# Packing four attention heads into TensorE, wider exponentials and hand-sliced background work in a two-layer attention and FFN kernel

## The chip, the cores and the metric

One core of one Trainium2 chip. The metric is the device time of one execution, in microseconds (us). Most executions of one kernel agree within 0.3%, those of the changed kernel within 0.5%; exceptions are named. Engines: PE is TensorE (PEld its weight loads), ACT is ScalarE, DVE is VectorE, POOL is GpSimd. PSUM is the memory that matmuls write to; a bank of it holds 512 columns here. The granted clock is the share of TensorE's full clock that the profile records; in all traces of this case the record is either 1 or 0.5. "Start to start" below is the distance between the starts of two neighbouring instructions of one engine; it is the cost of one of them in a full stream.

## The reference

```python
def _A_ref(x, wqkv, wo):            # S = 2048, D = 512, H = 32 heads of Dh = 16
    qkv = ...                       # x @ wqkv, split into q, k, v per head
    scores = jnp.einsum("bhqd,bhkd->bhqk", q, k) * Dh ** -0.5
    o = jnp.einsum("bhqk,bhkd->bhqd", _softmax(scores), v)
    return ... @ wo
def _B_ref(x, w1, w2):              # F = 1792
    return _silu(x @ w1) @ w2       # written as einsums
x = A_x
x = x + _A_ref(_layernorm(x), A_wqkv, A_wo)
x = x + _B_ref(_layernorm(x), B_w1, B_w2)
x = x + _A_ref(_layernorm(x), A_wqkv, A_wo)
x = x + _B_ref(_layernorm(x), B_w1, B_w2)
```

The heads have only 16 dimensions, so the scores and the weighted values of 32 heads fill little of a 128x128 array, while every score needs an exponential: 2 x 32 x 2048 x 2048 of them, 128 at a time.

## The kernel before

A query chunk is 512 tokens. For each pair of heads and each of 16 key tiles: two score matmuls (all 128 rows of the array; the query copy QJ has zeros in the rows of the other heads), one exponential of 1024 columns, two value matmuls whose weights are 128 columns wide, of which 17 are used (the 17th is a column of ones: the softmax sum).

```python
def emit_s(kt, ...):
    s_ps = psr.s_tile(kt % 2).rearrange("p (a b) -> p a b", a=2)
    for jj in range(2):
        nc.tensor.matmul(s_ps[:, jj, :], lhsT=KT[:, _hb, kt * P : (kt + 1) * P],
                         rhs=_qtj[:, jj, :], start=True, stop=True)
# [cut]
for kt in range(NKT):
    s_ps = s_tiles.pop(kt)
    p_sb = ppool.tile([P, 2, 512], BF16, name="p_sb", tag="p")
    nc.scalar.activation(p_sb[:]..., s_ps[:]..., ACT.Exp, scale=float(SCALE))
    if kt + 2 < NKT:
        emit_s(kt + 2)
    for jj in range(2):
        h = 4 * hb + 2 * pr + jj
        nc.tensor.matmul(o_ps[:, jj, :], lhsT=vaug[:, kt, 17 * h : 17 * h + P],
                         rhs=p_sb[:, jj, :], start=(kt == 0), stop=(kt == NKT - 1))
```

Projections, norms and the FFN of the chunk before are ordinary code; a scheduler interleaves them. The norms' square root runs on ACT in some places. A bound on each row's score is subtracted through an extra row (Bm, amax).

Of the kernel before, what the change touches and what calls it, by code (L numbers as in the profile page):

```python
# [8 lines left out]
ACT = mybir.ActivationFunctionType  # L9
ALU = mybir.AluOpType  # L10
AX = mybir.AxisListType
FP32 = mybir.dt.float32
BF16 = mybir.dt.bfloat16


@with_exitstack
def kernel(
# [11 lines left out]

# [4 lines left out]
    P = 128  # L34
    H = 32
    DH = D // H
    assert D == 512 and DH == 16, (D, DH)
    assert S % 512 == 0 and F % P == 0
    CT = D // P
    TT = S // P  # L40
    NQC = S // 512
    FT = F // P
    HB = H // 4
    NKT = TT
    SCALE = DH ** -0.5
    EPS = 1e-5

    cpool = ctx.enter_context(tc.tile_pool(name="cpool", bufs=1))
    wpool = ctx.enter_context(tc.tile_pool(name="wpool", bufs=1))
    xpool = ctx.enter_context(tc.tile_pool(name="xpool", bufs=1))  # L50
    xnpool = ctx.enter_context(tc.tile_pool(name="xnpool", bufs=4))
    xtpool = ctx.enter_context(tc.tile_pool(name="xtpool", bufs=4))
    qtpool = ctx.enter_context(tc.tile_pool(name="qtpool", bufs=2))
    qwork = ctx.enter_context(tc.tile_pool(name="qwork", bufs=1))
    ppool = ctx.enter_context(tc.tile_pool(name="ppool", bufs=3))
    otpool = ctx.enter_context(tc.tile_pool(name="otpool", bufs=1))
    achunk_pool = ctx.enter_context(tc.tile_pool(name="achunk", bufs=2))
    atpool = ctx.enter_context(tc.tile_pool(name="atpool", bufs=2))
    htpool = ctx.enter_context(tc.tile_pool(name="htpool", bufs=1))
    tpool = ctx.enter_context(tc.tile_pool(name="tpool", bufs=1))  # L60
    lnpool = ctx.enter_context(tc.tile_pool(name="lnpool", bufs=2))
    small = ctx.enter_context(tc.tile_pool(name="small", bufs=4))
    pspool = ctx.enter_context(tc.tile_pool(name="pspool", bufs=1, space=bass.MemoryType.PSUM))
    PSF = pspool.tile([P, 4096], FP32, name="PSF")
    PSBF = PSF[:].bitcast(BF16)

    class _PSRegions:
        def __init__(self):
            self.g_ctr = 0

        def s_tile(self, idx):
            return PSF[:, idx * 1024 : (idx + 1) * 1024]

        def o_tile(self):
            return PSF[:, 2048:3072].rearrange("p (a b) -> p a b", a=2)

        def att_tile(self):
            return PSBF[:, 4096:5120].rearrange("p (a b c) -> p a b c", a=4, b=2)

        def g_f32(self):  # L80
            i = self.g_ctr % 2
            self.g_ctr += 1
            return PSF[:, 3072 + 512 * i : 3072 + 512 * (i + 1)]

        def g_bf16_ct(self):
            i = self.g_ctr % 2
            self.g_ctr += 1
            base = 6144 + 1024 * i
            return PSBF[:, base : base + CT * P].rearrange("p (a b) -> p a b", a=CT)

    psr = _PSRegions()


    ident = cpool.tile([P, P], BF16, name="ident")
    make_identity(nc, ident[:])
    cw = cpool.tile([P, 768], BF16, name="cw")
    nc.vector.memset(cw[:], 0.0)
    nc.vector.memset(cw[0:1, 128:640], 1.0)
    for j in range(4):
        nc.vector.memset(cw[0:1, 32 * j + 16 : 32 * j + 17], 1.0)  # L100
        nc.vector.memset(cw[0:1, 640 + 32 * j : 640 + 32 * j + 16], 1.0)
    E = cpool.tile([P, P], BF16, name="E")
    nc.gpsimd.memset(E[:], 0.0)
    for j in range(4):
        nc.gpsimd.memset(E[32 * j : 32 * j + 16, 32 * j + 16 : 32 * j + 17], -1.0)
    eps_t = cpool.tile([P, 1], FP32, name="eps_t")
    nc.vector.memset(eps_t[:], EPS)

    onescol = cpool.tile([P, 1], FP32, name="onescol")
    maskcol = cpool.tile([P, 1], FP32, name="maskcol")  # L110
    mc_ps = psr.g_f32()
    nc.tensor.matmul(mc_ps[:, 0:1], lhsT=cw[0:1, 0:128], rhs=cw[0:1, 128:129], start=True, stop=True)
    nc.tensor.matmul(mc_ps[:, 2:3], lhsT=cw[0:1, 640:768], rhs=cw[0:1, 128:129], start=True, stop=True)
    nc.vector.tensor_copy(out=onescol[:], in_=mc_ps[:, 0:1])
    nc.vector.tensor_copy(out=maskcol[:], in_=mc_ps[:, 2:3])

    x_sb = xpool.tile([P, TT, D], BF16, name="x_sb")
    for c in range(NQC):
        nc.sync.dma_start(
            x_sb[:, 4 * c : 4 * c + 4, :],  # L120
            xf[512 * c : 512 * (c + 1), :].rearrange("(tt p) d -> p tt d", p=P),
        )

    wq_pad = wpool.tile([P, CT, HB, P], BF16, name="wq_pad")
    wk_pad = wpool.tile([P, CT, HB, P], BF16, name="wk_pad")
    wv_sb = wpool.tile([P, CT, D], BF16, name="wv_sb")
    wo_sb = wpool.tile([P, CT, D], BF16, name="wo_sb")
    w1_sb = wpool.tile([P, CT, F], BF16, name="w1_sb")
    w2_sb = wpool.tile([P, FT, D], BF16, name="w2_sb")

    def _qk_src(ct, col0):
        return bass.AP(
            tensor=A_wqkv.tensor,
            offset=A_wqkv.offset + (ct * P) * 3 * D + col0,
            ap=[[3 * D, P], [16, 32], [1, 32]],
        )

    for ct in range(CT):
        nc.sync.dma_start(
            out=wk_pad[:, ct, :, :].rearrange("p hb (j s) -> p (hb j) s", s=32),  # L140
            in_=_qk_src(ct, D),
        )
    for ct in range(CT):
        nc.sync.dma_start(
            out=wq_pad[:, ct, :, :].rearrange("p hb (j s) -> p (hb j) s", s=32),
            in_=_qk_src(ct, 0),
        )
    nc.sync.dma_start(
        wv_sb[:], A_wqkv[:, 2 * D : 3 * D].rearrange("(ct p) f -> p ct f", p=P)
    )  # L150
# [4 lines left out]
    KT = xpool.tile([P, HB, S], BF16, name="KT")  # L155
    VW = 17 * (H - 1) + P + 17
    VW = (VW + 31) // 32 * 32
    vaug = xpool.tile([P, TT, VW], BF16, name="vaug")
    nc.vector.memset(vaug[:, :, 16 * H : VW], 1.0)
    nc.vector.memset(  # L160
        vaug[:, :, 0 : 17 * H].rearrange("p t (h e) -> p t h e", e=17)[:, :, :, 16:17],
        1.0,
    )
    QJs = [
        [xpool.tile([P, 2, 512], BF16, name=f"QJ{pr}{b}") for b in range(2)]
        for pr in range(2)
    ]
    for pr in range(2):
        for b in range(2):
            nc.vector.memset(QJs[pr][b][:], 0.0)  # L170
    qj_ctr = [0, 0]
    Bm = xpool.tile([P, HB, P], BF16, name="Bm")
    amax = xpool.tile([P, HB], FP32, name="amax")
    amaxp = xpool.tile([P, HB, NQC], FP32, name="amaxp")
    hT = htpool.tile([P, FT, 512], BF16, name="hT")

    def ln_tiles(tts, act_sqrt=True):
        n = len(tts)
        mvb = lnpool.tile([P, n, 2], FP32, name="mvb", tag=f"mvb{n}")
        for i, tt in enumerate(tts):  # L180
            st = lnpool.tile([P, 6], FP32, name="st", tag="st", bufs=4)
            nc.vector.bn_stats(st[:], x_sb[:, tt, :])  # L182
            nc.vector.bn_aggr(mvb[:, i, :], st[:])  # L183
        rstd = lnpool.tile([P, n, 1], FP32, name="rstd", tag=f"rstd{n}")
        if act_sqrt:
            std = lnpool.tile([P, n, 1], FP32, name="std", tag=f"std{n}")
            nc.scalar.activation(  # L187
                std[:], mvb[:, :, 1:2], ACT.Sqrt, bias=eps_t[:], scale=1.0
            )
            nc.vector.reciprocal(rstd[:], std[:])  # L190
        else:
            a = lnpool.tile([P, n, 1], FP32, name="lna", tag=f"lna{n}")
            nc.vector.tensor_scalar_add(out=a[:], in0=mvb[:, :, 1:2], scalar1=float(EPS))
            r = lnpool.tile([P, n, 1], FP32, name="lnr", tag=f"lnr{n}")
            nc.vector.reciprocal(out=r[:], in_=a[:])
            rh = lnpool.tile([P, n, 1], FP32, name="lnrh", tag=f"lnrh{n}")
            nc.vector.tensor_scalar_mul(out=rh[:], in0=r[:], scalar1=0.5)
            nc.vector.tensor_scalar(
                out=rstd[:], in0=r[:], scalar1=1.0, scalar2=0.5, op0=ALU.add, op1=ALU.mult
            )  # L200
            rec = lnpool.tile([P, n, 1], FP32, name="lnrec", tag=f"lnrec{n}")
            t = lnpool.tile([P, n, 1], FP32, name="lnt", tag=f"lnt{n}")
            for _ in range(11):
                nc.vector.reciprocal(out=rec[:], in_=rstd[:])
                nc.vector.tensor_tensor(out=t[:], in0=rec[:], in1=rh[:], op=ALU.mult)
# [17 lines left out]
    def ln_chunk(qc, act_sqrt=True):  # L223
        return ln_tiles([4 * qc + i for i in range(4)], act_sqrt=act_sqrt)
# [371 lines left out]
```

## Time and profile before

| what | value |
|---|---|
| time, median of 12 runs | 2551.56 us (2549.15 to 2554.52) |
| PE busy, share of the span | 93% |
| ACT busy | 79% |
| exponentials | 2048 of 1024 columns, 1918 us, idle 362 us before them |
| granted clock | 0.991 |

How to read it: PE and ACT are idle little, and nearly tie. The question for the change is which of the two a removed piece of work belongs to, and what the other then does. The lines are in the prediction.

### The profile page before, as it was taken

How to read it: one execution, taken by the hardware profiler on the slowest of the kernel's cores; microseconds unless marked ns; L12 is line 12 of the kernel's file. 1: busy time of each engine (PE TensorE's matmuls, PEld its weight loads, DVE VectorE, ACT ScalarE, POOL GpSimd, SP SyncE). 2: the span in 40 equal slices, each digit the busy share in tenths (PEclk: the TensorE clock that was granted, in tenths of full speed). 3: DMA queues.
4: the chain of work that ended last, by engine and by line, in shares of the span. 5: the costliest groups of instructions: out<-in, count | busy, mean ns of one | idle time of the engine just before them, and what ended most of it. 6: DMA issues, size and time to landing. Idle time of an engine off the chain costs nothing.

```text
span 2551.0 us, 28923 instructions
## 1 busy us (share of the span) xinstructions
PE 2373.3 (93%) x11204; PEld 1054.8 (41%) x11426; DVE 828.3 (32%) x1841; ACT 2010.5 (79%) x2196; POOL 1.2 (0%) x11
## 2 busy tenths in 40 slices
PE   5999999999999989999689999999999999999997
PEld 2444444444444434444234444444444444344443
DVE  8233332312432142311573233423123411413124
ACT  1887789997789959999327877899968999499981
POOL 0000000000000000000000000000000000000000
PEclk9999999999999999999889999999999999999999
DMA  8000000000000000000000000000000000000000
GB/s 140 1 1 1 1 1 1 1 1 1 1 1 1 1 1 1 1 1 1 0 1 1 1 1 1 1 1 1 1 9 1 1 1 1 9 1 1 1 1 17
DMA packets 40650, 12.87 MB, mean 5 GB/s; under 512 B 33088, under 2 KB 40000, under 8 KB 40512
## 3 DMA queue, kind: packets, MB, share of 16 engines
q1 hardware_dynamic: 40512, 11.01, 2.3%
q8 instruction: 89, 1.46, 0.2%
q14 instruction: 49, 0.40, 0.1%
HBM read 8.91 MB, written 2.10 MB: 4 GB/s over the span
## 4 chain that ended last, share of the span: by engine, by line
PE 64%; ACT 21%; DVE 11%; issue 4%; ACTq 0%
PE PSF L354 26%; PE PSF L379 23%; ACT p_sb L369 20%; PE PSF L458 4%; PE PSF L296 2%; PE PSF L391 2%; PE PSF L437 2%; PE PSF L242 2%; DVE hT L446 1%; DVE st L182 1%; ACT t_sb L445 1%; PE PSF L420 1%; DVE oT L387 1%; PE PSF L281 1%; DVE KT L249 1%
## 5 line engine op out<-in xcount | busy, mean ns | idle before, releaser
L369 ACT ACTIVATE p_sb<-PSF 128x1024 bf16<-128x1024 f32 x2048 | 1918.1, 1044 | 362.1 <-PE PSF L354 283.9
L354 PE MATMUL PSF<-QJ,KT 128*128 128x512 bf16 x4034 | 1202.6, 378 | 41.8 <-ACT p_sb L369 22.7
L379 PE MATMUL PSF<-p_sb,vaug 128*128 128x512 bf16 x3970 | 1170.8, 378 | 5.7 <-ACT p_sb L369 0.3
L354 PEld LDWEIGHTS <-KT 128*128 128x128 bf16 x4096 | 396.4, 97 | 584.7 <-issue 272.4
L379 PEld LDWEIGHTS <-vaug 128*128 128x128 bf16 x4096 | 397.1, 97 | 490.8 <-issue 47.0
L387 DVE CAST oT<-PSF 128x1024 bf16<-128x1024 f32 x128 | 156.7, 1224 | 622.4 <-PE PSF L379 622.4
L344 DVE COPY QJ<-QT 17x512 bf16<-17x512 bf16 x256 | 72.7, 284 | 611.3 <-PE PSF L354 606.8
L437 PE MATMUL PSF<-xnT,w_sb 128*128 128x512 bf16 x442 | 135.5, 395 | 23.0 <-DVE hT L446 21.1
L445 ACT ACTIVATE t_sb<-PSF 128x512 f32<-128x512 f32 x112 | 67.2, 600 | 54.0 <-DVE hT L446 37.7
L458 PE MATMUL PSF<-w_sb,hT 128*128 128x512 bf16 x440 | 97.6, 379 | 3.5 <-DVE hT L446 3.1
L446 DVE SCALAR_TENSOR_TENSOR hT<-t_sb,PSF 128x512 bf16<-128x512 f32 x112 | 76.9, 687 | 56.1 <-ACT t_sb L445 55.7
L249 DVE TENSOR_SCALAR KT<-PSF,maskcol,onescol 128x512 bf16<-128x512 f32 x64 | 50.6, 807 | 125.0 <-PE PSF L242 124.5
L296 PE MATMUL PSF<-xnT,wq_pad 128*128 128x512 bf16 x246 | 73.0, 381 | 17.0 <-DVE qtmp L304 10.8
L391 PE MATMUL PSF<-ident,oT 128*128 128x128 bf16 x1024 | 78.4, 219 | 10.5 <-DVE oT L387 9.8
L242 PE MATMUL PSF<-xnT,wk_pad 128*128 128x512 bf16 x250 | 73.6, 397 | 14.3 <-DVE KT L249 6.8
L391 PEld LDWEIGHTS <-oT 128*128 128x128 bf16 x1024 | 65.1, 98 | 48.1 <-DVE oT L387 26.6
L187 ACT ACTIVATE std<-mvb,eps_t 128x4 f32<-128x4 f32 x16 | 4.8, 297 | 96.5 <-DVE mvb L183 96.5
L437 PEld LDWEIGHTS <-w_sb 128*128 128x128 bf16 x448 | 44.8, 100 | 86.3 <-issue 42.7
L231 PE MATMUL PSF<-ident,xn 128*128 128x128 bf16 x352 | 38.0, 252 | 42.1 <-DVE xn L212 33.1
L458 PEld LDWEIGHTS <-hT 128*128 128x128 bf16 x448 | 43.8, 98 | 57.3 <-issue 5.3
L304 DVE CAST qtmp<-PSF 128x512 bf16<-128x512 f32 x64 | 44.2, 690 | 48.8 <-PE PSF L296 45.7
L182 DVE BATCH_NORM_STATS2 st<-x_sb 128x6 f32<-128x512 bf16 x88 | 58.8, 676 | 0.4
(58 smaller groups left out, 660.6 us busy)
## 6 DMA issues: line engine op xcount, KB each, us to landing
w_sb<-in_B_w_dram SPq DMA_DIRECT2D x2, 1792.0 KB, 11.8
x_sb<-in_A_x_dram SPq DMA_DIRECT2D x4, 512.0 KB, 5.7
out_dram<-x_sb SPq DMA_DIRECT2D x4, 512.0 KB, 2.9
wk_pad<-in_A_wqkv_dram SPq DMA_DIRECT2D x4, 256.0 KB, 9.6
wq_pad<-in_A_wqkv_dram SPq DMA_DIRECT2D x4, 256.0 KB, 8.8
wv_sb<-in_A_wqkv_dram SPq DMA_DIRECT2D x1, 512.0 KB, 6.5
wo_sb<-in_A_wo_dram SPq DMA_DIRECT2D x1, 512.0 KB, 4.9
```

The lines of the kernel that those rows point to most:

```text
L182: nc.vector.bn_stats(st[:], x_sb[:, tt, :])
L242: nc.tensor.matmul(k_ps[:, :], lhsT=wk_pad[:, ct, hb, :], rhs=xnT[:, ct, :], start=(ct == 0), stop=(ct == CT - 1),)
L296: nc.tensor.matmul(q_ps[:, :], lhsT=wq_pad[:, ct, hb, :], rhs=xnT[:, ct, :], start=(ct == 0), stop=(ct == CT - 1),)
L354: nc.tensor.matmul(s_ps[:, jj, :], lhsT=KT[:, _hb, kt * P : (kt + 1) * P], rhs=_qtj[:, jj, :], start=True, stop=True,)
L369: nc.scalar.activation(p_sb[:].rearrange("p a b -> p (a b)"), s_ps[:].rearrange("p a b -> p (a b)"), ACT.Exp, scale=float(SCALE),)
L379: nc.tensor.matmul(o_ps[:, jj, :], lhsT=vaug[:, kt, 17 * h : 17 * h + P], rhs=p_sb[:, jj, :], start=(kt == 0), stop=(kt == NKT - 1),)
L387: nc.vector.tensor_copy(out=oT[:, :, :], in_=o_ps[:, :, :])
L391: nc.tensor.transpose(att_ps[:, tq, jj, :], oT[:, jj, tq * P : (tq + 1) * P], ident[:, :],)
L437: nc.tensor.matmul(h_ps[:, :], lhsT=w1_sb[:, ct, ft * P : (ft + 1) * P], rhs=xnT[:, ct, :], start=(ct == 0), stop=(ct == CT - 1),)
L445: nc.scalar.activation(t_sb[:], h_ps[:, :], ACT.Tanh, scale=0.5)
L446: nc.vector.scalar_tensor_tensor(out=hT[:, ft, :], in0=t_sb[:], scalar=1.0, in1=h_ps[:, :], op0=ALU.add, op1=ALU.mult,)
L458: nc.tensor.matmul(y_ps[:, :], lhsT=hT[:, ft, tq * P : (tq + 1) * P], rhs=w2_sb[:, ft, :], start=(ft == 0), stop=(ft == FT - 1),)
```

## The change

Intent: let neighbouring heads use different parts of the array at once, so that PE stops limiting, and let ACT run without a gap on wider instructions. Its core, cut, with remarks added after #:

```diff
+    NB = 3                                  # blocks of 512 columns per exponential
-                            lhsT=KT[:, _hb, kt * P : (kt + 1) * P],
-                            rhs=_qtj[:, jj, :],
+                r = slice(32 * j, 32 * j + 32)          # j: one of four row groups
+                    s_ps[:, i, :],                      # i: one of three banks
+                    lhsT=KT[L, kt // 4][r, g, (kt % 4) * P : (kt % 4 + 1) * P],
+                    rhs=QT[L, qc][r, g, par, :],
-                            o_ps[:, jj, :],
-                            lhsT=vaug[:, kt, 17 * h : 17 * h + P],
+                o_ps[32 * j : 32 * j + 32, :],          # one of four column groups
+                lhsT=VA[L, kt // 4][:, kt % 4, 17 * h : 17 * h + 32],
... [cut: pools; scores of tile t are issued, then values of tile t - 2, then the exponential of t]
+            if not (urgent or late):
+                if bg.queue:
+                    bg.pump()               # one slice of projection, norm or FFN work
+                else:                       # nothing to do: two dummy matmuls
+                    d_ps = ps_m.tile([P, 512], FP32, name="d_ps", tag="m")
+                    for _ in range(2):
+                        nc.tensor.matmul(d_ps[:], lhsT=ident[:], rhs=w1_sb[:, 0, 0:512], ...)
... [cut]
+    def m_tile(shape, dt, name):            # "burst": work that exponentials wait for
+        if burst[0]:                        # may use three rotating PSUM tiles
+            burst[1] += 1
+            if burst[1] % 3:
+                return ps_s.tile(shape, dt, name=name, tag="s")
+        return ps_m.tile(shape, dt, name=name, tag="m")
-            nc.scalar.activation(std[:], mvb[:, :, 1:2], ACT.Sqrt, bias=eps_t[:], scale=1.0)
+        nc.gpsimd.tensor_scalar_add(rstd[:], mv[:, :, 1:2], float(EPS))
+        nc.gpsimd.tensor_tensor(out=rstd[:], in0=rstd[:], in1=half[:], op=ALU.pow)
```

Below, a "tile" is one exponential with its score and value matmuls, and a "slice" is the piece of background work that one tile may carry (two matmuls or four transposes). When a group of four heads ends, the kernel finishes the background accumulation that is under way, because there is only one bank for both.

## The prediction

> **What bounds the kernel now.** I read the busy shares first, then the chain that ended last, then the costliest groups. These are the busy line, the chain's engines and the three large groups:
>
> ```profile
> PE 2373.3 (93%) x11204; PEld 1054.8 (41%) x11426; DVE 828.3 (32%) x1841; ACT 2010.5 (79%) x2196; POOL 1.2 (0%) x11
> ...
> PE 64%; ACT 21%; DVE 11%; issue 4%; ACTq 0%
> ...
> L369 ACT ACTIVATE p_sb<-PSF 128x1024 bf16<-128x1024 f32 x2048 | 1918.1, 1044 | 362.1 <-PE PSF L354 283.9
> L354 PE MATMUL PSF<-QJ,KT 128*128 128x512 bf16 x4034 | 1202.6, 378 | 41.8 <-ACT p_sb L369 22.7
> L379 PE MATMUL PSF<-p_sb,vaug 128*128 128x512 bf16 x3970 | 1170.8, 378 | 5.7 <-ACT p_sb L369 0.3
> ```
>
> Two engines are nearly tied. ScalarE's exponentials need 1918 us and idle 362 us, mostly waiting for the score matmuls; TensorE's busy time is 93% of the span. The timeline separates them. First ScalarE, then TensorE in a stretch of pure attention:
>
> ```profile
> 403.21 2.85 ACT L369 ACTIVATE p_sb<-PSF 128x1024 bf16<-128x1024 f32 x3 [0.26 <-PE PSF L354]
> ...
> 604.57 12.11 ACT L369 ACTIVATE p_sb<-PSF 128x1024 bf16<-128x1024 f32 x13 [0.38 <-PE PSF L379]
> ```
>
> ```profile
> 607.48 0.59 PE L354 MATMUL PSF<-QJ,KT 128*128 128x512 bf16 x2
> ...
> 607.91 0.59 PE L379 MATMUL PSF<-p_sb,vaug 128*128 128x512 bf16 x2
> ...
> 608.40 0.59 PE L354 MATMUL PSF<-QJ,KT 128*128 128x512 bf16 x2
> ```
>
> Three exponentials whose scores are ready take 2.85, so one costs (2.85 - 1.04)/2 = 0.903 us start to start. In the longer run it is (12.11 - 1.04)/12 = 0.922, because one step of TensorE, two score and two value matmuls, repeats every 0.92 us (607.48 to 608.40). A matmul costs (0.59 - 0.378) = about 0.215, so four cost 0.86: the tie. Any projection or FFN matmul put into such a step makes TensorE the bound, and that is where the 362 us of ScalarE idle time come from.
>
> Last, the stretches without attention: start, boundary between the layers, tail.
>
> ```profile
> 0.00:62.00 62.00, 35.34 (x175) 17.87 (x179) 54.97 (x141) 6.00 (x10) 1.17 (x11) 1.00 0.83 144
> ...
> 1205.00:1322.00 117.00, 87.13 (x405) 39.73 (x411) 75.76 (x166) 26.33 (x37) 0.00 (x0) 0.87 0.00 1
> ...
> 2476.00:2551.00 75.00, 54.87 (x249) 23.95 (x252) 31.98 (x57) 15.86 (x25) 0.00 (x0) 0.95 0.04 15
> ```
>
> Columns: stretch, length, busy time of PE, weight loads, DVE, ACT and POOL, granted clock, DMA share, GB/s. Together 254 us in which ScalarE works 48.
>
> **What the Trainium skill says.** (1) "ScalarE: Activation LUTs", What ACT_TABLE_LOAD costs: an ACTIVATE with immediate operands takes 186 ns + 0.833 ns per column, back-to-back ones overlap by 93 ns, and exp and tanh share a table set. The trace agrees on length (186 + 853 = 1039; measured 1044) and on the set (tables are reloaded only around the square root). The overlap is larger here: 1044 - 903 = 141 ns. So a start-to-start cost is about 50 ns + 0.833 per column. (2) "TensorE: Matmul & The Clock Gate", Part 3: a K=32 matmul takes as long as a K=128 one; the gain is concurrency of matmuls at different row groups (four gave 3.07x) or at different column groups (three gave 2.38x). No matmul of the kernel before is packed, so its trace cannot confirm it. (3) "TensorEngine Tiling (Array Packing)", Key Properties: changing the tiling mode drains the engine. Not shown before either. (4) The first of these TensorE pages, Part 1: an idle window of about 3.4 us halves the clock. The boundary's 0.87 agrees.
>
> **The change part by part.** The change rewrites the kernel; the arithmetic of the attention stays 4096 blocks (8 chunks x 32 heads x 16 key tiles) of 128x512 scores.
>
> Exponentials: 2048 instructions of 1024 columns become 1365 of 1536 and one of 512. By (1): 50 + 1280 = 1.33 us each, 1365 x 1.33 + 0.5 = 1816 us, against 2048 x 0.903 = 1849 if before had never waited. So wider instructions give only 33 us; the rest must come from ScalarE no longer waiting.
>
> TensorE: each score matmul now uses 32 rows (keys of one head, zeros masked in the query), three neighbours at three row groups into three banks; each value matmul has 32 columns, three neighbours at different column groups of one bank. Packed by (2), a triple should cost about its full length, 0.38 + 0.01. With a drain after scores, values and background by (3), a tile costs 0.39 + 0.39, plus a background step of two matmuls (0.215 + 0.378 = 0.59): 1.37 us at worst, equal to an exponential; without a background step 0.78. Background matmuls: K and Q now handle eight heads instead of four, so 256 + 256 become 128 + 128, and the 64 of the bound (Bm) vanish; V, output and FFN keep 128 + 128 + 896. That is 1408 instead of 1728. Transposes (eight in a row took 0.61 us, 0.08 each) fall from 1504 to 640. In total per tile (1408 x 0.215 + 640 x 0.08)/1366 = 0.26 us on average, so TensorE has room.
>
> Background work in slices: each tile pumps one slice (two matmuls or eight transposes). I count per chunk about 12 slices for the output projection, 79 for the FFN, 25 for the next layer's LN, K and V, 12 for Q, with their gaps, and some 20 tiles where a group's end takes the place: 148 of the 171 tiles. So it fits, with few idle slots (there the dummy matmuls run). 84 of 112 tanh land between exponentials, 0.05 + 0.427 = 0.48 each: 40 us.
>
> VectorE: the absolute maximum (42 us), the |q| and bound operations (44 + 48) and the QJ copies (73) go; output casts become 64 of 512 columns (0.69 each) for 128 of 1.224. Far from the bound. LN's square root goes to a power on GpSimd: 20 table loads of 1.28 us become one, mostly in the boundary anyway.
>
> Start: before, the first exponential starts at 58.6 us, after K weights arrive in 64-byte pieces and after LN of all chunks. Now one x chunk, then one wide weight transfer (estimate 11 us, from the 11.8 that 1792 KB took), LN of one chunk about 6 us beside it, K, Q, V: first exponential at about 20. Chunks 1 to 3 still need LN, K and V (about 9 us of VectorE: 2.6 statistics, 1.4 normalising, 1.5 copies, 5 x 0.69) before their keys; two tiles of exponentials hide some: 3 x 8 = 24 us lost.
>
> Boundary: layer 2 starts on the three finished chunks, and after 16 tiles needs the fourth's FFN, LN, K and V in one burst. The FFN's first half now costs 1.41 us per group of 128, as in the tail:
>
> ```profile
> 2521.30 1.02 PE L437 MATMUL PSF<-xnT,w_sb 128*128 128x512 bf16 x4 [0.39 <-DVE hT L446]
> ...
> 2521.34 0.60 ACT L445 ACTIVATE t_sb<-PSF 128x512 f32<-128x512 f32 x1 [0.81 <-DVE hT L446]
> ...
> 2521.97 0.69 DVE L446 SCALAR_TENSOR_TENSOR hT<-t_sb,PSF 128x512 bf16<-128x512 f32 x1 [0.72 <-ACT t_sb L445]
> ...
> 2522.71 1.02 PE L437 MATMUL PSF<-xnT,w_sb 128*128 128x512 bf16 x4 [0.39 <-DVE hT L446]
> ```
>
> With three rotating PSUM tiles instead of two, the 0.39 wait should shrink: 14 x 1.0 = 14, second half 56 x 0.215 = 12, two LN of 6 to 7, K and V 8 x 0.87 = 7, less two hidden tiles: about 45 us. Tail: output projection 7, LN 6, 14 + 12, last add and store 4, group end 2: about 45.
>
> Sum: 20 + 1816 + 40 + 24 + 45 + 45 = 1990. Add 64 group ends at about 0.2 (13) and about 700 matmul slices that each overrun ScalarE by 1.37 - 1.33 = 0.04 (28): 2031 us, ratio 0.796.
>
> **The rivals.** Rival A, no concurrency: triples run one after another at 0.215. Then TensorE needs (8192 + 1408) x 0.215 + 51 = 2115, plus dummies in perhaps 160 tiles (70) and 60 to 80 us in which it is idle at the ends: about 2260. For: no trace here shows packing. Against: the skill's measured ratios, and operands that start at partitions 0, 32, 64, 96. Even so faster by 11%.
> Rival B, drains and weight loads cost more than I gave, say 0.25 us more per tile: TensorE becomes the bound in the about 900 tiles with slices and loses 0.25 x 900 = 220 us, about 2220. For: three mode changes per tile. Against: the score tiles are made a whole exponential ahead, so slices with gaps give time back.
> Rival C, the clock halves because of gaps: a tile costs 2.7, span far above 2551 if permanent. Against: TensorE would be idle less than 1 us at a time, and the dummies fill empty slots; only the burst and the tail (LN) are exposed, some 10 us.
> Rival D, everything is absorbed better than I think (no group end cost, no overrun, shorter bursts): 1960.
>
> **Range and chances.** Mine and D hold about 75%, A and B together 20%, C 3%. Predicted 2030, 8 in 10 between 1960 and 2150. A loss of all gain needs C or something unseen: faster 0.95, within 2% 0.02, slower 0.03.
>
> **What would show it.** Right: exponentials of 128x1536 with a mean near 1.46 us, 1.33 apart, their idle time falling from 362 to about 150 us, nearly all in start, boundary and tail; ScalarE above 90% of the span; three score matmuls starting within about 0.1 us of each other; chain led by ACT. Wrong: score starts 0.215 apart (A); gaps before value matmuls and exponentials waiting for scores in ordinary tiles (B); granted clock well under 0.95 outside the ends (C); first exponential long after 20 us or a boundary above 60 us (my sums of the serial parts).

## The result, and the profile after

The changed kernel takes 2085.2 us (median of 8 runs, 2082.64 to 2093.21). The ratio is 0.8174 (95% interval 0.8164 to 0.8184). Ratios here are the mean time of one kernel's fast runs over the mean time of the other's fast runs in the same rounds, so not quite the ratio of the medians.

From the page after, the busy line, the clock row (tenths of full speed, 40 slices of the span), the chain by engine, and the four large groups:

```profile
PE 1739.8 (84%) x11072; PEld 586.2 (28%) x11266; DVE 415.4 (20%) x746; ACT 1904.1 (92%) x1479; POOL 36.4 (2%) x47
...
PEclk8999998889989899999979999999998999989999
...
ACT 56%; issue 23%; PE 16%; DVE 4%; POOL 1%; DMA 0%; ACTq 0%; POOLq 0%
...
L496 ACT ACTIVATE p_sb<-s_ps 128x1536 bf16<-128x1536 f32 x1366 | 1861.7, 1735 | 120.8 <-PE s_ps L479 120.3
L479 PE MATMUL s_ps<-QT,KT 32*128 32x512 bf16 x4096 | 564.1, 400 | 221.3 <-ACT p_sb L496 155.2
L420 PE MATMUL o_ps<-p_sb,VA 128*32 128x512 bf16 x4096 | 587.3, 411 | 1.6 <-DVE oT L429 1.4
L508 PE MATMUL d_ps<-w_sb,ident 128*128 128x512 bf16 x944 | 293.4, 385 | 0.0
```

ACT now leads the chain and is 92% busy; its idle time before exponentials fell from 362 to 121 us. The same 4096 score and 4096 value matmuls keep PE busy for 564 and 587 us in place of 1203 and 1171. The last line is the dummies: 293 us of work that computes nothing. And the clock row is no longer all 9: its mean is 0.934 against 0.991.

An ordinary tile on PE, with dummies, in layer 2:

```profile
1137.81 0.39 PE L479 MATMUL s_ps<-QT,KT 32*128 32x512 bf16 x3
...
1138.13 0.40 PE L420 MATMUL o_ps<-p_sb,VA 128*32 128x512 bf16 x3
...
1138.46 0.61 PE L508 MATMUL d_ps<-w_sb,ident 128*128 128x512 bf16 x2
...
1139.15 0.39 PE L479 MATMUL s_ps<-QT,KT 32*128 32x512 bf16 x3
```

Three packed matmuls together last as long as one (0.39). The three scores of a tile start within 0.01 us of each other, in all tiles of this trace: the packing does run them at once. The next kind starts 0.32 us after them, not 0.215 after as a matmul of the same kind does: about 0.11 us is lost at each change of shape. What in the change costs this, no run separates. Two full-array dummies take 0.54 (the weight loads of the next scores are recorded at 1139.00; the scores themselves then wait for the exponential until 1139.15). On ACT:

```profile
367.57 4.34 ACT L496 ACTIVATE p_sb<-s_ps 128x1536 bf16<-128x1536 f32 x3
371.56 0.84 ACT L329 ACTIVATE t_sb<-h_ps 128x512 f32<-128x512 f32 x1
372.05 4.59 ACT L496 ACTIVATE p_sb<-s_ps 128x1536 bf16<-128x1536 f32 x3
```

Three exponentials from 367.57 to 371.56 are 1.33 us each, start to start, and a tanh adds 0.49. By stretch (columns as in the prediction):

```profile
0.00:22.00 22.00, 9.18 (x43) 4.43 (x44) 12.73 (x32) 1.60 (x2) 3.92 (x10) 1.00 0.93 329
22.00:80.00 58.00, 45.11 (x250) 18.32 (x253) 34.82 (x61) 30.01 (x23) 9.56 (x9) 0.74 0.04 11
80.00:1037.00 957.00, 810.15 (x5244) 264.26 (x5333) 185.93 (x328) 932.75 (x718) 13.36 (x15) 0.93 0.00 1
1037.00:1094.00 57.00, 41.59 (x183) 18.90 (x184) 31.69 (x55) 10.44 (x17) 4.45 (x5) 0.79 0.00 0
1094.00:2033.00 939.00, 799.60 (x5197) 264.42 (x5286) 126.55 (x232) 920.22 (x710) 3.80 (x6) 0.96 0.01 3
2033.00:2081.00 48.00, 34.22 (x166) 15.91 (x168) 23.66 (x41) 9.07 (x16) 1.27 (x2) 0.89 0.04 12
```

In the two long stretches, 1896 us together, ACT is idle for 43 us by these counts; start, first chunk, boundary and tail are where ACT waits long.

The span can be summed from the start times on ACT. The first exponential starts at 21.7; 1365 steps of 1.331 are 1817; 84 tanh at 0.48 are 40; the three later x chunks cost 28; the layer boundary costs 57; the last exponential to the end is 48. That is 2012. The other 68 us are intervals above 1.331 in ordinary tiles. I sorted those by whether the score matmuls around them took 0.39 or 0.61: 34 us lie at the long ones, where the clock was halved, 30 us at full clock, most of it at the ends of head groups, and 4 us are intervals under 0.1 us over. The sort is not sharp. By the clock's own records 26 us lie in intervals that are wholly at half clock, 20 us in wholly full ones and 21 us in ones in which the clock changes; and some 38 us, at either clock, lie where a group ends. So the two causes overlap, and 34 and 30 are rough. A tile at half clock, with a slice:

```profile
369.28 0.61 PE L479 MATMUL s_ps<-QT,KT 32*128 32x512 bf16 x3
...
369.82 0.61 PE L420 MATMUL o_ps<-p_sb,VA 128*32 128x512 bf16 x3
...
370.37 1.03 PE L319 MATMUL h_ps<-fT,w_sb 128*128 128x512 bf16 x2
```

Scores and values are now 0.54 apart and the slice takes 0.97, about 2.05 in all: more than the 1.33 of an exponential, so ACT waits. As the clock is either full or half, a mean of 0.934 means (1 - 0.934)/0.5 = 13% of the span at half, about 275 us.

### The profile page after: what moved, and what is told of

It is laid out like the page before. It is cut to its first block, busy times and chain, and to the rows that moved or that the text cites. A ratio compares the mean times of both kernels' runs of the same rounds, so it can differ in the third digit from the quotient of the medians.

```text
span 2080.8 us, 26171 instructions
## 1 busy us (share of the span) xinstructions
PE 1739.8 (84%) x11072; PEld 586.2 (28%) x11266; DVE 415.4 (20%) x746; ACT 1904.1 (92%) x1479; POOL 36.4 (2%) x47
## 4 chain that ended last, share of the span: by engine, by line
ACT 56%; issue 23%; PE 16%; DVE 4%; POOL 1%; DMA 0%; ACTq 0%; POOLq 0%
ACT p_sb L496 53%; PE s_ps L479 3%; PE o_ps L420 3%; PE h_ps L319 3%; ACT t_sb L329 3%; PE f_ps L343 2%; PE t_ps L186 2%; DVE st L161 1%; PE v_ps L244 1%; PE k_ps L206 1%; DVE xn L172 1%; PE att L262 1%; POOL rstd L167 0%; DVE hT L330 0%; PE q_ps L223 0%
## 5 line engine op out<-in xcount | busy, mean ns | idle before, releaser
L496 ACT ACTIVATE p_sb<-s_ps 128x1536 bf16<-128x1536 f32 x1366 | 1861.7, 1735 | 120.8 <-PE s_ps L479 120.3
L479 PE MATMUL s_ps<-QT,KT 32*128 32x512 bf16 x4096 | 564.1, 400 | 221.3 <-ACT p_sb L496 155.2
L420 PE MATMUL o_ps<-p_sb,VA 128*32 128x512 bf16 x4096 | 587.3, 411 | 1.6 <-DVE oT L429 1.4
L479 PEld LDWEIGHTS <-KT 32*128 32x128 bf16 x4096 | 230.8, 91 | 699.9 <-issue 643.4
L508 PE MATMUL d_ps<-w_sb,ident 128*128 128x512 bf16 x944 | 293.4, 385 | 0.0
L420 PEld LDWEIGHTS <-VA 128*32 128x32 bf16 x4096 | 141.3, 94 | 338.4 <-issue 332.5
L319 PE MATMUL h_ps<-fT,w_sb 128*128 128x512 bf16 x410 | 133.4, 425 | 32.7 <-DVE hT L330 27.3
L330 DVE SCALAR_TENSOR_TENSOR hT<-t_sb,h_ps 128x512 bf16<-128x512 f32 x112 | 77.1, 688 | 325.5 <-ACT t_sb L329 325.5
L343 PE MATMUL f_ps<-w_sb,hT 128*128 128x512 bf16 x420 | 119.2, 384 | 4.3 <-issue 2.1
L329 ACT ACTIVATE t_sb<-h_ps 128x512 f32<-128x512 f32 x112 | 75.3, 672 | 40.5 <-PE h_ps L319 40.5
```

Source lines behind the costliest of these rows:

```text
L319: nc.tensor.matmul(h_ps[:], lhsT=w1_sb[:, ct, ft * P : (ft + 1) * P], rhs=fT[:, ct, :], start=(ct == 0), stop=(ct == CT - 1),)
L329: nc.scalar.activation(t_sb[:], h_ps[:], ACT.Tanh, scale=0.5)
L330: nc.vector.scalar_tensor_tensor(out=hT[:, ft, :], in0=t_sb[:], scalar=1.0, in1=h_ps[:], op0=ALU.add, op1=ALU.mult,)
L343: nc.tensor.matmul(y_ps[:], lhsT=hT[:, ft, tq * P : (tq + 1) * P], rhs=w2_sb[:, ft, :], start=(ft == 0), stop=(ft == FT - 1),)
L420: nc.tensor.matmul(o_ps[32 * j : 32 * j + 32, :], lhsT=VA[L, kt // 4][:, kt % 4, 17 * h : 17 * h + 32], rhs=p_sb[:, i, :], start=(kt == 0) ...
L479: nc.tensor.matmul(s_ps[:, i, :], lhsT=KT[L, kt // 4][r, g, (kt % 4) * P : (kt % 4 + 1) * P], rhs=QT[L, qc][r, g, par, :], start=True, sto ...
```

## The experiments

The theory to test (P): packing took PE off the path and ACT's stream now sets the time. The rival (W): the wider exponentials and the slicing did it, and packing is a detail. The second question is the 68 us. Theory F puts it down to the halved clock where gaps lack matmuls; rival H puts it down to the group ends. Times are medians of four runs (five or twelve where said), beside the kernel before on the same chip. Where a kernel computes wrong numbers, that was on purpose.

**1. Scores and values on the full array, all else kept** (wrong numbers).

```diff
-                    lhsT=KT[L, kt // 4][r, g, (kt % 4) * P : (kt % 4 + 1) * P],
-                    rhs=QT[L, qc][r, g, par, :],
+                    lhsT=KT[L, kt // 4][:, g, (kt % 4) * P : (kt % 4 + 1) * P],
+                    rhs=QT[L, qc][:, g, par, :],
-                o_ps[32 * j : 32 * j + 32, :],
-                lhsT=VA[L, kt // 4][:, kt % 4, 17 * h : 17 * h + 32],
+                o_ps[:, :],
+                lhsT=VA[L, kt // 4][:, kt % 4, 17 * min(h, 25) : 17 * min(h, 25) + P],
-                start=(kt == 0),
-                stop=(kt == NKT - 1),
+                start=(kt == 0 and j == 0),
+                stop=(kt == NKT - 1 and j == 3),
```

> The changed kernel with every score matmul on 128 rows and every value matmul on 128 columns (wrong numbers on purpose; one accumulation group per bank), all else kept, the fillers too. Theory P (the packing is what took TensorE off the path): a tile then costs six matmuls of 0.215 = 1.29 us and a slice or filler 0.43, 1.72 in most tiles, so TensorE is the bound and the time is about 2400 us (2300 to 2450). Rival W (the wider exponentials and the slicing brought the gain, packing is a detail): it stays within 2% of the changed kernel, about 2085.

Measured: 2443.56 us, ratio 0.9578 to the kernel before, clock 0.994. In the timeline of this run a tile on PE is:

```profile
1700.56 0.81 PE L478 MATMUL s_ps<-QT,KT 128*128 128x512 bf16 x3
1701.21 0.81 PE L420 MATMUL o_ps<-p_sb,VA 128*128 128x512 bf16 x3
1701.86 0.60 PE L343 MATMUL f_ps<-w_sb,hT 128*128 128x512 bf16 x2
1702.29 0.81 PE L478 MATMUL s_ps<-QT,KT 128*128 128x512 bf16 x3
```

From 1700.56 to 1702.29 are 1.73 us, as worked out. W as stated is out, and P holds in kind: without packing PE is the bound again, and 358 of the 466 us gained are gone. The size is not the worth of packing alone, though, for the dummies stayed in, and on a PE that is the bound they cost time. The exponentials of this run show it: in 512 tiles with dummies they start 1.725 us apart on average (in the timeline, scores at 1300.47 and 1302.19), in 166 tiles with neither slice nor dummy 1.335, as fast as ACT can go. Without dummies the run would take about 2443 - 512 x 0.39 = 2243 us; this is an estimate, it takes the clock to stay near 0.99 without them as in the kernel before, and the run was not made. By it packing is worth about 160 us here, and all the rest of the change (width, slices, fewer projections and transposes, shorter start and boundary, square root) about 310.

**2 and 3. Each half alone** (the corresponding lines of the diff above; wrong numbers).

> Only the score matmuls on 128 rows, values still packed. Theory P: scores 0.65 us, values 0.32, slice 0.54: 1.5 us in tiles with a slice or filler, 0.97 without; between 2120 and 2250 us. Rival W: about 2085. It also tells whether the three score matmuls are really concurrent now: if not, nothing changes.

> Only the value matmuls on 128 columns, scores still packed. Theory P: the same as for the scores, 2120 to 2250 us; the two halves should be worth about the same, and each alone less than half of both together, because ScalarE's 1.33 us hides the first part. Rival W: about 2085.

Measured: 2208.34 and 2207.35 us, clocks 0.991 and 0.987. Both are in the stated range and equal to each other. Each alone costs 123 or 122 us and both cost 358, so the costs do not add: ACT hides the first part. In each of the two, about 90 us of the loss lie in tiles with dummies.

**4. The kernel before with packing alone.**

```diff
-                            lhsT=KT[:, _hb, kt * P : (kt + 1) * P],
-                            rhs=_qtj[:, jj, :],
+                            lhsT=KT[32 * (2 * pr + jj) : 32 * (2 * pr + jj) + 32, _hb, kt * P : (kt + 1) * P],
+                            rhs=QT[32 * (2 * pr + jj) : 32 * (2 * pr + jj) + 32, _hb, :],
-                            o_ps[:, jj, :],
-                            lhsT=vaug[:, kt, 17 * h : 17 * h + P],
+                            o_ps[32 * jj : 32 * jj + 32, :],
+                            lhsT=vaug[:, kt, 17 * h : 17 * h + 32],
... [cut: the query copies go; the output cast and its transposes take 64 partitions]
```

> The kernel before with one part of the change alone: its score matmuls on 32 rows each (two heads of a pair at two row groups) and its value matmuls on 32 columns (two column groups of one bank), without the zero-padded query copies; exponentials still 1024 wide, order still the scheduler's. Theory P: ScalarE then bounds the attention at 0.905 us an exponential: 1850 + 40 tanh + 10 table loads in the middle, plus the unchanged 254 us of start, boundary and tail, so 2155 to 2200 us, ratio about 0.85: most of the gain from packing alone. Rival W: above 2450 us, as packing does not matter.

Measured: 2766.58 us, correct, ratio 1.0845: slower than the kernel before, by 8.5%, with a granted clock of 0.664. P as I had stated it falls: packing alone does not bring most of the gain, it loses. Its timeline in plain attention:

```profile
604.47 0.60 PE L338 MATMUL PSF<-QT,KT 32*128 32x512 bf16 x2
...
605.00 0.61 PE L363 MATMUL PSF<-p_sb,vaug 128*32 128x512 bf16 x2
...
605.54 0.61 PE L338 MATMUL PSF<-QT,KT 32*128 32x512 bf16 x2
```

Each pair takes 0.54 before the next can start, so a step is 1.07 to 1.08 us. At full clock two pairs would need 0.64, and at 0.905 ACT would be the bound. The pairs do run together (0.54, where two one after the other would take 0.86 at this clock without any change of shape); that the clock is what is missing is tested in experiment 7.

**5. The changed kernel without its dummies.**

```diff
-                else:
-                    d_ps = ps_m.tile([P, 512], FP32, name="d_ps", tag="m")
-                    for _ in range(2):
-                        nc.tensor.matmul(d_ps[:], lhsT=ident[:], rhs=w1_sb[:, 0, 0:512], ...)
```

> The changed kernel without its dummy matmuls. Theory F (gaps without matmuls let the granted clock halve, and that costs time only where a slice of background work meets a halved clock): the granted clock falls from 0.93 to 0.7 to 0.8, but a tile without a slice needs only 0.54 + 0.54 us at half clock, less than 1.33, so the time rises by at most 1.5%, 2085 to 2115 us. Rival G (the clock is needed everywhere): above 2150 us.

Measured: 2107.19 us, ratio 0.8256, clock 0.738. As F said: at half clock scores and values need 1.08 us, which the 1.33 us of a wide exponential hides. The dummies are worth about 22 us.

**6. Two blocks per exponential, no dummies** (`NB = 3` becomes `NB = 2`, on top of experiment 5).

> Two blocks per exponential (1024 columns) in place of three, and no dummies (to be read against the run without dummies). Theory P: ScalarE's part rises by only 2048 x 0.905 - 1366 x 1.331 = 35 us, but TensorE's fixed spacing of 0.32 per packed group now counts 2048 times: 0.32 + 0.32 + 0.54 with a slice is 1.18, more than 0.905, in about 1000 tiles, partly given back by the others: 2150 to 2300 us. Rival W (the width is what matters through ScalarE's fixed cost alone): 35 us over the run without dummies.

Measured: 2714.21 us as median, but its four runs spread from 2629.34 to 2759.88 and only the fastest counts as fast, so there is no interval; even that one is 522 us above experiment 5. Both theories missed, by more than 300 us even on the fast run. In a stretch with attention and little else:

```profile
1500.00:1700.00 200.00, 198.49 (x748) 39.67 (x746) 8.24 (x18) 184.77 (x181) 0.00 (x0) 0.50 0.00 1
```

PE is busy 198 of 200 us and the granted clock is 0.50. This profile is of a slow run, but experiment 4, whose runs are all fast, shows the same:

```profile
400.00:700.00 300.00, 289.04 (x1123) 67.26 (x1129) 49.77 (x96) 239.04 (x242) 0.00 (x0) 0.59 0.00 1
```

So the clock is halved although PE, as recorded, hardly stands idle. A tile needs 1.08 us, more than ACT's 0.905, PE is the bound, and being the bound does not bring the clock back.

**7. Experiment 4 plus one useless full-array matmul per step.** A new theory, K: packed matmuls count for little in what decides the granted clock.

```diff
                     if kt + 2 < NKT:
                         emit_s(kt + 2)
+                    nc.tensor.matmul(
+                        PSF[:, 2560:3072], lhsT=ident[:, :], rhs=w1_sb[:, 0, 0:512],
+                        start=True, stop=True,
+                    )
```

> The kernel before with packed attention matmuls, as in the run that came out 8% slower at a granted clock of 0.66, and now one useless full-array matmul of 512 columns added in each of its 2048 steps. Theory K (the clock is granted by how much of the array works, packed matmuls count for little, and that run was slow because its clock was halved): the clock rises above 0.9, a step costs about 0.32 + 0.32 + 0.3, near ScalarE's 0.905, and the kernel gets FASTER by work added: 2200 to 2400 us. Rival I (the clock fell because TensorE idles between its waits, or packing is slow by itself): the clock stays below 0.75, the time rises above 2766.

Measured (12 runs): 2552.47 us, clock 0.989, ratio to the kernel before 0.9994. Adding 2048 matmuls made experiment 4's kernel 214 us faster. The direction is K's, and rival I is out; the size is not, since I had said 2200 to 2400. Its timeline:

```profile
604.55 0.39 PE L338 MATMUL PSF<-QT,KT 32*128 32x512 bf16 x2
604.87 0.39 PE L367 MATMUL PSF<-p_sb,vaug 128*32 128x512 bf16 x2
605.19 0.39 PE L361 MATMUL PSF<-w_sb,ident 128*128 128x512 bf16 x1
605.51 0.39 PE L338 MATMUL PSF<-QT,KT 32*128 32x512 bf16 x2
```

Full clock, three groups of 0.32: 0.96 us a step, over ACT's 0.905, and every projection or FFN matmul comes on top. PE is still the bound, as before the change. Even a single matmul occupies 0.32 between two changes of shape.

**8. Two blocks per exponential, dummies kept** (`NB = 2` alone).

> The changed kernel with two blocks per exponential and its dummies kept, one size changed. Theory K: with dummies in the empty slots the clock is kept (above 0.85), but a tile with slice or dummy needs 0.32 + 0.32 + 0.54 = 1.18 us of TensorE against ScalarE's 0.905, so TensorE bounds: 2300 to 2500 us, far below the 2714 of two blocks without dummies. Rival W (only ScalarE's fixed cost counts): 2120 us.

Measured: 2728.28 us (2708.4 to 2740.04), ratio 1.0675, clock 0.901. A miss: K was right on the clock but I expected a gain over experiment 6, and there is none. In the 1158 tiles with dummies the dummies cost more than the clock gives: 0.32 + 0.32 + 0.54 = 1.18 a tile, against 1.08 at half clock without them. The 667 tiles with slices take 1.48 on average; in the first of these two stretches, which has many of them, the clock is often half:

```profile
300.00:500.00 200.00, 195.79 (x779) 42.79 (x778) 30.73 (x54) 145.19 (x149) 1.26 (x2) 0.68 0.00 1
...
1500.00:1700.00 200.00, 196.15 (x1003) 50.90 (x1002) 11.07 (x22) 170.75 (x168) 0.00 (x0) 0.98 0.00 1
```

The one size, three blocks to two, costs 643 us. In the account of the prediction it was worth 33.

**9. The square root back on ACT** (five runs).

```diff
-        nc.gpsimd.tensor_scalar_add(rstd[:], mv[:, :, 1:2], float(EPS))
-        nc.gpsimd.tensor_tensor(out=rstd[:], in0=rstd[:], in1=half[:], op=ALU.pow)
+        std = small.tile([P, 4, 1], FP32, name="std", tag="std")
+        nc.scalar.activation(std[:], mv[:, :, 1:2], ACT.Sqrt, bias=eps_t[:], scale=1.0)
+        nc.vector.reciprocal(rstd[:], std[:])
```

> The reciprocal root of the layer norms on ScalarE (Sqrt and a VectorE reciprocal) instead of the power on GpSimd: one part undone. If ScalarE bounds the stream, each of the 12 layer norms between exponentials adds two table loads of 1.28 us and a 0.3 us activation, 2.9 us, less what already stood idle: 25 to 40 us more, 2110 to 2125 us. Rival: hidden in ScalarE's waits, within 8 us of 2085.

Measured: 2115.35 us, ratio 0.8292, about 30 us more. The profile lists 32 table loads of 1.283 us, 41 us, where the changed kernel has one. About two thirds of what is added to ACT (40 us of loads, 5 of square roots) reappear in the time, as they should where ACT is the bound.

**10. Bursts in one PSUM bank.**

```diff
-            if burst[1] % 3:
+            if False:
```

> The changed kernel whose bursts (start, boundary, tail) use one PSUM bank in place of three rotating ones. My account of the serial stretches: an FFN group then costs 0.86 + 0.60 + 0.69 = 2.2 us in place of 0.87, 14 of them at the boundary and 14 at the end: 2 x 18 us, K and V some 0.7 us more each, about 30 of them: 20 us; 2085 + 55 = 2130 to 2150 us. Rival: those stretches are bound by VectorE's norms alone, within 15 us of 2085.

Measured: 2211.47 us, ratio 0.866, clock 0.907. My account was right in kind and too small: 126 us, not 45 to 65. In the burst at the boundary the FFN groups of 128 are 3.27 us apart (tanh at 1081.14 and 1084.41), not 2.2, because the four matmuls of a group now take 1.87 us: between the waits for the bank the clock stays halved. So the rotation, by shortening the waits, also keeps more of these stretches at full clock.

**11. Dummies in the tiles where the background pauses.**

```diff
+            if gap:
+                for _ in range(2):
+                    nc.tensor.matmul(
+                        s_ps[:, 0, :], lhsT=ident[:], rhs=w1_sb[:, 0, 0:512], start=True, stop=True
+                    )
```

> Two dummy matmuls also in the tiles where the background pauses (written to the score bank ahead of the scores, which overwrite it). Theory F: the 68 us that exponentials lose in ordinary tiles (intervals above 1.331 outside start, boundary and tail) come mostly from halved-clock windows, 277 us of them; with the pauses filled the halved time falls below 120 us, the loss below 40, and the time to 2040 to 2060 us. Rival H (the loss comes from group ends and drains, the clock only accompanies it): the clock improves but the time stays within 10 us of 2085, or rises.

Measured: 2077.56 us, ratio 0.8134 (0.8123 to 0.8145), clock 0.959. A small gain, 8 us, where F had said 25 to 45. By the clock about 170 us are still halved, and the loss in ordinary tiles is still 63 us. By the marks set beforehand this is H (within 10 us of 2085) and every mark of F is missed. But the halved time fell only from 277 to about 170, not below 120, so F was not fully put to the test: the pauses are only part of the tiles without full-array matmuls. About half of the loss lies at group ends, which dummies do not touch.

**12. A version meant to beat both.** Dummies in every tile without background matmuls; statistics of a norm taken right after each residual add; memory sets of the value tiles moved to the start and to each chunk's end; dummies during the norms of the boundary and the tail; and no FFN output accumulation begun within 7 tiles of a group's end. The two edits that matter for the verdict:

```diff
+            if pe[0] == 0 and t > 60:
+                filler(s_ps[:, 0, :], 2)
+            pe[0] = 0
+            near[0] = 21 - (NB * t % 64) // NB
... [cut: the rest]
+            while near[0] < 7 and not bg.forced:
+                yield 0
```

> A version meant to beat both: fillers in every tile without background matmuls; no FFN output accumulation begun within 7 tiles of a group's end (a group's end has to finish it at once); norm statistics taken right after each residual add; the memory sets of the value tiles moved away from the norms; dummies during the norms of the boundary and the tail. Expected from the parts: cold losses 34 to about 10, group ends 30 to about 15, boundary 57 to 48, tail 48 to 42: about 2085 - 55 = 2030 us (2020 to 2055). If group ends and the clock are not what the 68 us in ordinary tiles are made of, it stays above 2065.

Measured: 2076.26 us, correct, ratio 0.8132 (0.812 to 0.8144), clock 0.982. It beats the changed kernel by 0.5% and misses its own target. The boundary cost 48 us, as hoped. By the mark set beforehand (above 2065) group ends and clock would not be what the 68 us are made of. The trace speaks for another reading: less of the loss lies in intervals with a mean clock under 0.75 (about 14 us, against 40 in the changed kernel), but the ordinary tiles lost 77 us, more than before the mending, and ten intervals of 4.5 to 4.8 us make 34 of them. One is here; the first line is from PE, the second, in its own view, from ACT:

```profile
900.43 2.76 PE L382 MATMUL f_ps<-w_sb,hT 128*128 128x512 bf16 x12
```

```profile
905.12 5.58 ACT L546 ACTIVATE p_sb<-s_ps 128x1536 bf16<-128x1536 f32 x4 [3.22 <-PE s_ps L529]
```

The end of a group forces the open accumulation to be finished at once: 12 matmuls in a row, and ACT waits 3.22 us. My rule counted the tiles by their scores, but the end comes two to three tiles later, with the values. So the rule let accumulations begin just as the old group was about to end, the worst moment. That is my slip. These ten intervals show what closing an accumulation costs; that the same makes up the group-end loss of the changed kernel is likely, but a corrected rule was not run.

## Why the prediction was right, and where its steps were off

The time lies in the range, 54 us over the point. By its steps:

- **Exponentials**: 1816 us predicted, 1817 measured at 1.331 each. Tanh 40, measured 40. First exponential 20, measured 21.7. These held. Only the check that I named for them was bad: the recorded mean length is 1.735 us, not 1.46, although starts are 1.33 apart. In a long back-to-back run the records stretch; the start times carry the rate.
- **TensorE packed**: triples 0.39 apart predicted, 0.32 measured, and 1.18 in place of 1.37 for a tile with a slice. So my 28 us for overruns were not needed at full clock. At half clock a tile with a slice took 2.05. My "eight transposes" a slice was a slip: the code issues four. The sign held by experiments 1 to 3: it is the packing that takes PE off the path in tiles with a slice.
- **Ordinary tiles**: 13 + 28 = 41 us predicted, 68 measured, but of other stuff: by a rough sort half at halved clock and half at group ends, where an open accumulation is closed at once. That the 28 us stood in for part of it was luck. This term and the next carry the miss.
- **Boundary and tail**: 45 and 45 predicted, 57 and 48 measured. The boundary's norms took 8.5 us (1037.6 to 1046.1) and 10.1 us (1073.34 to 1083.46), each with the add before it, rather than 6 to 7. In the second, one of the four normalisations took 2.03 us in place of 0.41: it ran beside a GpSimd memory set of a value tile (1.97 us), and so did all eight such cases in the trace. The first FFN groups and K projections ran at half clock after the norms (the stretch's clock is 0.79). FFN groups then came 0.87 apart, better than my 1.0. The three early chunks cost 28, not 24.
- **"Wider instructions give only 33 us"**: wrong. I had counted only ACT's fixed cost. Two blocks in place of three cost 643 us (experiment 8) or 522 (the fast run of 6 against 5). A packed group occupies 0.32 us of PE whether it holds one, two or three blocks, and 0.54 at half clock. With three blocks per tile, two groups and a slice (1.18) hide behind 1.33 us at full clock; with two blocks they exceed 0.905, and so do two groups alone at half clock (1.08).
- **Idle slots**: "few"; 148 of 171 predicted full. In fact 1026 dummy matmuls were loaded, so 513 of 1366 tiles had nothing to do, where the count leaves 184. It was near in chunks 2 to 4 of layer 1 (30, 32 and 38 such tiles for 23); it left out that the first chunk of each layer has little to do beside it (96 and 130 idle tiles), and that layer 2 has no next layer to prepare (56, 61 and 70). Harmless, since ACT is the bound. Rival A with these dummies is 2443 us (experiment 1), not 2260; without them it would be about 2243 by the estimate there, so the 2260 was no bad guess.
- **Rival C**, halved clock, got 3% and the words "TensorE would be idle less than 1 us at a time". That criterion failed: PE 99% busy with packed matmuls had a clock of 0.50 (experiment 6). The sign named for C, a clock well under 0.95 outside the ends, did not appear, with 0.93 and 0.96 in the two long stretches, but it was near. The changed kernel spends about 13% of its span at half clock and pays only some 34 us in ordinary tiles, because three blocks per exponential leave room for it: 1.08 for scores and values, against 1.33.

So the right number rests on the right bound, ACT, and on a safeguard, the width, that I had read as a side matter; that the range held although I did not count on it was luck. (The dummies, the other safeguard, are worth 22 us.) What stays open is what the clock's grant counts. Experiments 4, 6 and 7 show that it is not busy time as recorded; whether it is active rows and columns, the gaps at each change of shape, or something else, no run here separates. How the remaining 68 us would shrink with a correct group-end rule, and how fast the kernel is with neither packing nor dummies, is also open.

## What to carry to other kernels

Packing small matmuls saves array time, but each change of shape had a fixed cost here (about 0.11 us) and packed matmuls alone did not keep the clock (0.50 and 0.59 with PE over 96% busy), so packing pays where a group is large against that cost and either full-array work runs beside it or another engine's time hides the half clock. Before judging a matmul change, read the granted clock next to the busy share: PE busy all the time may be PE at half clock. And when a part is taken out to see its worth, ask what else in the kernel was there only for that part: here the dummies. And a part that seems worth little by itself (here the width of an instruction) may be what lets another part pay.

## What the Trainium skill lacked or had wrong

- "TensorE: Matmul & The Clock Gate", Part 1, ties the full clock to how busy PE has been. The runs show PE busy 198.49 of 200 us with packed matmuls at a granted clock of 0.50, and 0.664 rising to 0.989 when 2048 full-array matmuls were added. The page says of transposes that they do not count as busy in the same way; it says nothing like it of packed matmuls. The runs show only that recorded busy time, whose ends are modelled, is not what counts; short gaps at the changes of shape may still be behind it.
- The same page, Part 3, gives 3.07x for four row groups and 2.38x for three column groups. Between changes of shape the three-fold packing gave 0.65/0.32 = 2.0x here for scores and values alike.
- "TensorEngine Tiling (Array Packing)", Key Properties, says that a mode change drains the engine, without a number. Here groups start 0.32 us apart where matmuls of one kind start 0.215 apart, so about 0.11 us a change at full clock, and also 0.11 at half (0.54 against 0.43).
- "ScalarE: Activation LUTs", What ACT_TABLE_LOAD costs, gives 93 ns of overlap between ACTIVATEs. Measured start to start: 0.903 us for 1024 columns and 1.331 for 1536, so by its length formula (1039 and 1466 ns) overlaps of 136 and 135.
- No page says that the profile's recorded length of back-to-back ACTIVATEs stretches: mean 1.735 us at a start-to-start rate of 1.331.
